# One hand-ordered schedule for a decode layer with its gradients: FFN weights read once in blocks, wo and K/V kept on chip, zero fills released step by step

## The chip, the cores and the metric

The kernel runs on one core of a Trainium2 chip. The metric is device time in microseconds, from runs of the whole program; the profile shows one execution of it. The core has five instruction queues that run side by side, each in its own order: TensorE (PE, with its weight loads as PEld), VectorE (DVE), ScalarE (ACT), GpSimd (POOL) and SyncE (SP). SP, ACT and POOL can issue DMA transfers between memory and the on-chip buffer; all of them run on the core's 16 DMA engines.

## The reference

One token passes a layer: modulation from `c`, attention of 32 query heads over the last 4096 rows of a cache with 4 K/V heads, a gated FFN. The outputs are the layer's output and the gradients of all inputs. Two of these, for the caches, have the size of the whole caches (65536 rows each), and are zero but for the last 4096 rows.

```python
W = min(4096, max(256, Sk // 4))
q = (x @ wq).reshape(B, Sq, Hq, Dh)
k = k_cache[:, :, Sk - W:, :] ; v = v_cache[:, :, Sk - W:, :]   # each K/V head serves 8 query heads
p = softmax(q k^T * Dh ** -0.5) ; o = p v
return o.reshape(B, Sq, Hq * Dh) @ wo                            # A_ref

h = sigmoid(x @ w_gate) * (x @ w_up)
return h @ w_down                                                # B_ref

sa, ca, ga, sb, cb, gb = (silu(c) @ w_mod).reshape(6, D)
h = layernorm(x) * (1 + ca) + sa ; x = x + ga * A_ref(h)
h = layernorm(x) * (1 + cb) + sb ; x = x + gb * B_ref(h)
# outputs: x, and the gradients of x, k_cache, v_cache, wq, wo, w_gate, w_up, w_down, c, w_mod
```

All is bfloat16. D is 1024, F 3584, wq 1024 x 4096, wo 4096 x 1024, w_mod 1024 x 6144.

## The kernel before

With one token there is hardly arithmetic: each weight is read, multiplied with a vector, and a gradient of its size, an outer product of two vectors, is written. A vector of 1024 stands as a column tile of 128 partitions x 8. Products with weights in the forward pass go to TensorE, with the weight as the stationary operand and one column as the moving one. Products in the backward pass (weight times gradient, summed along the rows) go to VectorE as one multiply-and-sum over a weight tile and a vector broadcast to all partitions: the helper `ttr` (L207), whose elementwise result goes to a scratch tile `junk`. The outer products are `outer_rows` (L211), also on VectorE, into staging tiles of the pool `stage` (2 buffers), which SP then stores. `bcast_from_col` (L202) makes the broadcast vectors: VectorE multiplies the identity with each column into `diag` (L200), TensorE multiplies with ones, ScalarE copies the result out of PSUM (L204).

The kernel's operations are written in the order of the layer; a scheduler orders each engine's queue from that, and pools decide which buffer a tile gets. The stages:

- POOL issues the 120 zero fills for the caches' gradients (L110), 1 MB each, at the start and one behind the other; eight may be in flight. Behind them in its queue stand small memsets, `dhh` (L405) among them.
- Modulation: w_mod in three tiles, 384 matmuls (L234). Query: wq in 8 tiles, 256 matmuls (L267).
- K is loaded and transposed (L297, copies L298), scores (L311), softmax, transposed probabilities (L336), V, output (L348). Then wo and 256 matmuls (L372), second norm.
- FFN: all of w_down (`wd`) and w_gate (`wg`) is loaded into the four slots of the pool `big`; the reductions of w_down (L207), 224 matmuls with w_gate (L423). w_up (`wu_t`) is streamed in 8 row tiles through 2 buffers (L441): matmuls (L444), reduction, outer product, store (L450). Then the w_gate reductions with their outer products (stored at L470), matmuls with w_down (L476), w_down's outer products (L486).
- Backward norm, four of the six w_mod sections (`wmod_section`, load L515, store L525), each reading its 1024 columns of w_mod again.
- wo is read again (`wo_r`), reduced, its gradient written (L545). K and V are read again (`k_sb2`, `v_sb2`), V transposed, gradients of V (L566, L570, stored at L574), the scores' gradient in two passes (L581, L589), gradients of K, the query's gradient (L348).
- wq is read again (`wqr`, L607), reduced, its gradient written (L616); backward norm; the last two w_mod sections.

## Time and profile before

| | us |
|---|---|
| median of 3 runs | 846.26 |
| lowest and highest run | 846.24 and 846.75 |
| span of the profiled execution, first to last instruction | 844.5 |
| DVE busy in it | 360.4 |
| PE busy | 173.9 |
| ACT busy | 101.8 |
| POOL busy | 65.4 |

The profile shows one execution. Its page gives the span in 40 equal slices (21.1 us each); a digit is the busy share of an engine in tenths, the row of the DMA engines gives their mean busy share, and the row under it what they moved in GB/s. A group row names line, engine, operation, output and inputs with their shapes, and after the bar the group's busy time, the mean duration of one in ns and the idle time before it with what ended it. A row of the timeline has its start and duration first. A window's row gives, behind its two times and its length, the busy time and count of PE, PEld, DVE, ACT and POOL, then TensorE's clock, the DMA engines' busy share and GB/s. The issue table gives for each group of transfers the size of one and the median time from issue to landing.

### The profile page before, as it was taken

The numbers are of one execution on the slowest core, as the hardware profiler recorded it, in microseconds if no ns is written. First come the engines' busy times: TensorE is split into PE (matmuls) and PEld (weight loads), VectorE is DVE, ScalarE is ACT, GpSimd is POOL, SyncE is SP. The second block draws the span as 40 slices with busy tenths as digits, with TensorE's granted clock in tenths as the row PEclk, the third lists the DMA queues.
The fourth block names the chain that finished last, engine by engine and source line by source line (L and its number), as shares of the span: only waits on it lengthen the run. The fifth ranks groups of instructions, "written<-read, shape, count | busy, mean of one in ns | idle before, by whom it ended". The sixth has DMA issues, their size and how long they took to land. (4 is left out here: it accounts for less than half of the span.)

```text
span 844.5 us, 7215 instructions
## 1 busy us (share of the span) xinstructions
PE 173.9 (21%) x2932; PEld 130.3 (15%) x2932; DVE 360.4 (43%) x680; ACT 101.8 (12%) x161; POOL 65.4 (8%) x136
## 2 busy tenths in 40 slices
PE   0211028310003000021002124021000057980032
PEld 0211025210003000021001123010000046560011
DVE  1100000300001000000399889997899940549986
ACT  0000006600000000000001001000100049460000
POOL 3111111111111111111100000000000000000000
PEclk9999999655555555555555555555555556555555
DMA  8999999999999999999931966888989996873423
GB/s 345 424 424 425 427 426 424 423 423 423 422 424 421 424 422 425 427 425 425 427 133 34 329 247 243 324 291 308 335 300 346 338 366 236 336 258 153 195 101 149
DMA packets 64749, 283.60 MB, mean 336 GB/s; under 512 B 4294, under 2 KB 4294, under 8 KB 43212
## 3 DMA queue, kind: packets, MB, share of 16 engines
q1 hardware_dynamic: 47436, 157.31, 49.5%
q0 software_dynamic: 17280, 125.84, 35.3%
q8 instruction: 23, 0.38, 0.2%
q14 instruction: 10, 0.08, 0.0%
HBM read 97.52 MB, written 185.60 MB: 335 GB/s over the span
## 5 line engine op out<-in xcount | busy, mean ns | idle before, releaser
L110 POOL DMA_DIRECT2D out_dram<-zeros x120 | 63.8, 533 | 348.6 <-DMA out_dram<-zeros 342.1
L207 DVE CUSTOM_DVE_ANT_0 junk<-wm_sec,dmod_b 128x1024 bf16<-128x1024 bf16 x48 | 58.4, 1218 | 2.8 <-ACT dmod_b L204 2.8
L202 PE MATMUL bc_ps<-diag,ones_bf 128*128 128x128 bf16 x152 | 31.1, 266 | 121.0 <-DVE diag L200 105.4
L456 DVE TENSOR_SCALAR omsg<-sg 128x28 f32<-128x28 f32 x1 | 0.2, 181 | 116.5 <-ACT sg L426 116.5
L207 DVE CUSTOM_DVE_ANT_0 junk<-wd,dffn_b 128x1024 bf16<-128x1024 bf16 x28 | 34.3, 1224 | 33.0 <-POOL dhh L405 32.2
L207 DVE CUSTOM_DVE_ANT_0 junk<-wo_r,dattn_b 128x1024 bf16<-128x1024 bf16 x32 | 38.8, 1211 | 0.0
L375 DVE COPY attn_col<-attn_ps 128x8 f32<-128x8 f32 x1 | 0.2, 167 | 87.3 <-PE attn_ps L372 87.3
L207 DVE CUSTOM_DVE_ANT_0 junk<-wqr,dq_b 128x4096 bf16<-128x4096 bf16 x8 | 35.3, 4417 | 1.1 <-issue 1.1
L202 PEld LDWEIGHTS <-ones_bf 128*128 128x128 bf16 x152 | 14.0, 107 | 133.3 <-issue 114.0
L207 DVE CUSTOM_DVE_ANT_0 junk<-wu_t,du_b 128x3584 bf16<-128x3584 bf16 x8 | 31.1, 3891 | 5.4 <-DMA wu_t<-in_B_w_up_dram 4.4
L207 DVE CUSTOM_DVE_ANT_0 junk<-wg,dg_b 128x3584 bf16<-128x3584 bf16 x8 | 31.1, 3883 | 0.4 <-ACT dg_b L204 0.4
L423 PE MATMUL g_ps<-h_bf,wg 128*128 128x1 bf16 x224 | 7.4, 166 | 110.5 <-DMA wg<-in_B_w_gate_dram 108.5
L298 ACT COPY kT_sb<-tp_kv 128x1024 bf16<-128x1024 bf16 x16 | 15.4, 1017 | 100.2 <-PE tp_kv L297 100.1
L566 PEld LDWEIGHTS <-P_bf 8*128 8x128 bf16 x256 | 25.1, 133 | 7.2 <-issue 4.6
L211 DVE TENSOR_SCALAR dwm_stg<-dmod_b,cs_col 128x1024 bf16<-128x1024 bf16 x48 | 22.6, 480 | 5.5 <-DMA out_dram<-dwd_stg 5.5
L204 ACT CAST dmod_b<-bc_ps 128x512 bf16<-128x512 f32 x12 | 6.7, 587 | 149.5 <-PE bc_ps L202 101.4
L372 PE MATMUL attn_ps<-o_bf,wo 128*128 128x1 bf16 x256 | 8.1, 166 | 79.6 <-DMA wo<-in_A_wo_dram 79.6
L423 PEld LDWEIGHTS <-wg 128*128 128x128 bf16 x224 | 6.7, 104 | 111.2 <-DMA wg<-in_B_w_gate_dram 109.2
L298 ACT COPY vT_sb<-tp_kv 128x1024 bf16<-128x1024 bf16 x16 | 15.3, 1028 | 65.5 <-PE tp_kv L297 65.5
L237 DVE COPY mod_col<-mod_ps 128x48 f32<-128x48 f32 x1 | 0.2, 208 | 51.5 <-PE mod_ps L234 51.5
L581 DVE CUSTOM_DVE_ANT_0 junk<-sc_ps,P_bf 128x512 bf16<-128x512 f32 x8 | 5.5, 692 | 35.3 <-PE sc_ps L311 34.3
L234 PE MATMUL mod_ps<-cs_bf,wm 128*128 128x1 bf16 x384 | 11.0, 165 | 46.1 <-DMA wm<-in_w_mod_dram 45.1
(190 smaller groups left out, 417.0 us busy)
## 6 DMA issues: line engine op xcount, KB each, us to landing
out_dram<-zeros POOLq DMA_DIRECT2D x120, 1024.0 KB, 25.7
wm<-in_w_mod_dram SPq DMA_DIRECT2D x6, 2048.0 KB, 34.4
wm_sec<-in_w_mod_dram SPq DMA_DIRECT2D x12, 1024.0 KB, 7.0
out_dram<-dwm_stg SPq DMA_DIRECT2D x12, 1024.0 KB, 5.0
wq<-in_A_wq_dram SPq DMA_DIRECT2D x8, 1024.0 KB, 44.9
k_sb<-in_A_k_cache_dram SPq DMA_DIRECT2D x8, 1024.0 KB, 23.5
v_sb<-in_A_v_cache_dram SPq DMA_DIRECT2D x8, 1024.0 KB, 18.9
wo<-in_A_wo_dram SPq DMA_DIRECT2D x8, 1024.0 KB, 49.6
```

The lines of the kernel that those rows point to most:

```text
L110: ins = zq.dma_start(out=region[:, i * ZW:i * ZW + w_], in_=zeros[:, :w_])
L202: nc.tensor.matmul(ps[:, jj * P:(jj + 1) * P], lhsT=ones_bf[:, :], rhs=dg_[:, :], start=True, stop=True)
L204: nc.scalar.copy(out=out_bf[:, j0 * P:(j0 + nj) * P], in_=ps[:, 0:nj * P])
L207: nc.vector.tensor_tensor_reduce(out=junk[:, 0:n], in0=w_ap, in1=b_ap, scale=1.0, scalar=0.0, op0=ALU.mult, op1=ALU.add, accum_out=acc_ap)
L211: nc.vector.tensor_scalar(out=stage_ap, in0=b_ap, scalar1=scal_ap, scalar2=None, op0=ALU.mult)
L234: nc.tensor.matmul(mod_ps[:, cidx:cidx + 1], lhsT=wm_sb[s][:, j, cc * P:(cc + 1) * P], rhs=cs_bf[:, j:j + 1], start=(j == 0), stop=(j == K ...
L237: nc.vector.tensor_copy(out=mod_col, in_=mod_ps[:, 0:KM])
L298: nc.scalar.copy(out=dst[:, g, tb * 1024:(tb + 1) * 1024], in_=tp[:, :])
L372: nc.tensor.matmul(attn_ps[:, cidx:cidx + 1], lhsT=wo_sb[h // 16][:, h % 16, cidx * P:(cidx + 1) * P], rhs=o_bf[:, h:h + 1], start=(h == 0 ...
L423: nc.tensor.matmul(g_ps[:, cidx:cidx + 1], lhsT=wg_j(j)[:, cidx * P:(cidx + 1) * P], rhs=h2_bf[:, j:j + 1], start=(j == 0), stop=(j == KD ...
L566: nc.tensor.matmul(ps[:, tt * DH:(tt + 1) * DH], lhsT=rows_bf[32 * g:32 * g + HG, t_ * P:(t_ + 1) * P], rhs=R_hd[32 * g:32 * g + HG, :], s ...
L581: nc.vector.tensor_tensor_reduce(out=junk[:, 0:512], in0=ps[:, 0:512], in1=P_bf[:, ch * 512:(ch + 1) * 512], scale=1.0, scalar=0.0, op0=AL ...
```

## The change

The kernel is written anew, in one order that the scheduler keeps (`manual_schedule`): each queue holds its instructions in the order of the code. Tiles have fixed places in one buffer, the arena.

- **Zero fills.** `zero(n, after)` puts the next `n` fills into POOL's queue, and each waits for the instruction `after` besides. There are 4 at the start, 38 more up to the FFN (after parts of the products with w_mod, wq and wo, and the transposes), 3 in each of the 7 FFN blocks, and 57 behind.
- **FFN in 7 blocks of 512 columns of F.** For each, one 1 MB tile of w_down, w_up and w_gate is loaded into five slots used in turn. Rows of the w_up and w_gate tiles are 1 KB in memory, those of w_down 8 KB. Forward and backward of a block follow each other: matmuls, sigmoids, reductions, broadcast, gradients. The reduction writes its elementwise result over the weight tile, the outer product over that, and the tile is stored from where it stands. The outer products of w_up and w_gate go to ScalarE (`outer_act`), which also issues their stores.
- **wo, K and V stay on chip.** Their second reads are gone; so is that of one of wq's 8 tiles. V's transposes take the place of K's in the forward pass.
- **w_mod** is read twice as before; in the backward pass in row tiles of 4096 columns through two slots, between the tiles of wq and behind them, and in tiles of 2048 columns at the end.
- **Smaller things.** The broadcast uses the column itself, repeated, as stationary operand, so that `diag` is gone. The memsets on POOL are gone. The scores' gradient is made in one pass, its row constant being taken from the outputs instead of the scores. The three input rows are loaded as one tile, the result rows are made with one transpose each.

Three places show what moved. The first is POOL's queue. Before, from the first fill on (`DMASW` are the semaphores of transfers issued by POOL, eight of them in turn):

```order
L110 DMA out_dram<-zeros 128x4096 [waits DVE_49]
L110 DMA out_dram<-zeros 128x4096 x7
L110 DMA out_dram<-zeros 128x4096 [waits DMASW0_49]
L110 DMA out_dram<-zeros 128x4096 [waits DMASW1_49]
L110 DMA out_dram<-zeros 128x4096 [waits DMASW2_49]
```

After, the fills of the first two FFN blocks and the first of the third:

```order
L119 DMA out_dram<-zeros 128x4096 [waits DMASW2_49,DVE_49]
L119 DMA out_dram<-zeros 128x4096 [waits DMASW3_49,Activation_49]
L119 DMA out_dram<-zeros 128x4096 [waits DMASW4_49,Activation_49]
L119 DMA out_dram<-zeros 128x4096 [waits DMASW5_49,DVE_49]
L119 DMA out_dram<-zeros 128x4096 [waits DMASW6_49,Activation_49]
L119 DMA out_dram<-zeros 128x4096 [waits DMASW7_49,Activation_49]
L119 DMA out_dram<-zeros 128x4096 [waits DMASW0_49,DVE_49]
```

Before, a fill waits only for the one eight places ahead of it. After, it waits for an instruction of another engine too.

The second is SP's queue in the FFN. Before, loads of w_up and stores of its gradient (`DMAHW` are the semaphores of transfers issued by SP and ACT):

```order
L441 DMA wu_t<-in_B_w_up_dram 128x3584 [waits DMAHW0_49,DMAHW2_49,DVE_49,PE_49]
L450 DMA out_dram<-dwu_stg 128x3584 [waits DMAHW3_49,DVE_49]
L441 DMA wu_t<-in_B_w_up_dram 128x3584 [waits DMAHW1_49,DMAHW4_49,DVE_49,PE_49]
L450 DMA out_dram<-dwu_stg 128x3584 [waits DMAHW5_49,DVE_49]
L450 DMA out_dram<-dwu_stg 128x3584 [waits DMAHW6_49,DVE_49]
L441 DMA wu_t<-in_B_w_up_dram 128x3584 [waits DMAHW7_49,DMAHW2_49,PE_49]
```

After, the store of a block's w_down gradient (L476), the loads of the next block's w_down, w_up and w_gate (L415, L418, L421), and the same for the block behind:

```order
L476 DMA out_dram<-arena 128x4096 [waits DMAHW6_49,DMAHW4_49,DVE_49]
L415 DMA arena<-in_B_w_down_dram 128x4096 [waits DMAHW5_49,DMAHW1_49,Activation_49]
L418 DMA arena<-in_B_w_up_dram 128x8x512 [waits DMAHW3_49,Activation_49]
L421 DMA arena<-in_B_w_gate_dram 128x8x512 [waits DMAHW4_49,DMAHW0_49,PE_49]
L476 DMA out_dram<-arena 128x4096 [waits DMAHW5_49,DMAHW2_49,DVE_49]
L415 DMA arena<-in_B_w_down_dram 128x4096 [waits DMAHW6_49,Activation_49]
L418 DMA arena<-in_B_w_up_dram 128x8x512 [waits DMAHW1_49,Activation_49]
L421 DMA arena<-in_B_w_gate_dram 128x8x512 [waits DMAHW2_49,PE_49]
```

The three loads now stand behind a store that waits for VectorE, and the load of w_gate waits for that store's landing as well, since it takes its slot.

The third is VectorE's queue in the FFN. Before, the last reduction with w_gate and its outer product, and the first outer products of w_down:

```order
L207 ISA junk_109,dh2g_2587<-wg1_1853,dg_b_2488 128x3584
L207 ISA dh2g_2587 128x1
L211 TENSOR_SCALAR dwg_stg_2618<-dg_b_2488,h2_1773 128x3584
L471 TENSOR_TENSOR dh2_2188<-dh2u_2189,dh2g_2587 128x8
L139 CAST x2_orow_2894<-ps_x2_0_2895 1x512
L211 TENSOR_SCALAR dwd_stg_2849<-dffn_b_1780,hh_2479 128x1024 x4
```

After, block 1 from its last reduction with w_down to the first one with w_up (`b1k` is the broadcast gradient, `dug` holds the gradients at the up and gate products):

```order
L151 ISA junk_1731,dhh1_1975<-arena_70,b1k_1710 128x1024
L151 ISA dhh1_1975 128x1
L134 TENSOR_TENSOR dug1_2016<-dhh1_1975,sg1_1971 128x4
L134 TENSOR_TENSOR dug1_2016<-dug1_2016,gu_ps_1906 128x4
L134 TENSOR_TENSOR dug1_2016<-dug1_2016,om1_1972 128x4
L143 CAST dug_bf1_2020<-dug1_2016 128x8
L147 TENSOR_SCALAR arena_70<-b1k_1710,hh1_1978 128x1024 x4
L151 ISA arena_70,dh2acc_1730<-arena_70,du_b_1732 128x512
L151 ISA dh2acc_1730 128x1
```

The outer products of w_up and w_gate are gone from this queue; the small products that need the block's sigmoids stand between the reductions.

The core of the diff:

```diff
-    for og in (out_2, out_3):
-        for g in range(G):
-            region = og[0, g, 0:SKW, :].rearrange("r d -> (r d)").rearrange("(p x) -> p x", p=P)
-            for i in range(nz):
-                ins = zq.dma_start(out=region[:, i * ZW:i * ZW + w_], in_=zeros[:, :w_])
+    def dep(later, earlier):
+        tc.add_manual_dep(later.ins, earlier.ins.name,
+                          mybir.DependencyInfo(mybir.DependencyClass.Sync, mybir.DependencyReason.DATA),
+                          reason="pace")
+    def zero(n, after=None):
+        for _ in range(n):
+            if not zleft:
+                return
+            ins = nc.gpsimd.dma_start(out=zleft.pop(0), in_=zeros[:, :])
+            if after is not None:
+                dep(ins, after)
...
-    for j in range(KD):
-        wu_t = stream.tile([P, F], BF16, tag="wstream", name="wu_t")
-        ld.dma_start(out=wu_t, in_=wu_view[:, j, :])
...
-        ttr(wu_t[:, :], du_b[:, :], dh2u[:, j:j + 1], F)
-        stg = stage.tile([P, F], BF16, tag="stg", name="dwu_stg")
-        outer_rows(stg, h2[:, j:j + 1], du_b[:, :])
-        st.dma_start(out=dwu_view[:, j, :], in_=stg)
+    def slot(i):
+        return ar(F_OFF + 8 * (i % 5), 8)
+    wd_t = [slot(3 * n) for n in range(NB)]
+    wu_t = [slot(3 * n + 1).rearrange("p (j f) -> p j f", j=KD) for n in range(NB)]
+    wg_t = [slot(3 * n + 2).rearrange("p (j f) -> p j f", j=KD) for n in range(NB)]
+    for n in range(NB):
...
+        for half, w in ((1, wu), (0, wg)):
+            for jj in range(4):
+                for j in range(KD):
+                    nc.tensor.matmul(gu[:, half * 4 + jj:half * 4 + jj + 1], lhsT=w[:, j, jj::4],
+                                     rhs=h2_bf[:, j:j + 1], start=(j == 0), stop=(j == KD - 1))
+        nc.scalar.activation(out=sg, in_=gu[:, 0:4], func=ACT.Sigmoid)
...
+        last = cp(dug_bf, dug)
+        zero(1, last)
...
+        for jj in range(4):
+            outer_dve(wd[:, jj, :], hh[:, jj:jj + 1], b1k)
+        nc.sync.dma_start(out=wd_dram(out_8, n), in_=wd_t[n])
+        for j in range(KD):
+            ttr(wu[:, j, :], wu[:, j, :], du_b, dh2acc[:, n * 16 + j:n * 16 + j + 1])
+            last = outer_act(wu[:, j, :], h2[:, j:j + 1], du_b)
+        nc.scalar.dma_start(out=dwu_view[:, :, n * FB:(n + 1) * FB], in_=wu)
+        zero(1, last)
+        if n + 1 < NB:
+            if n + 1 > 1:
+                load_wd(n + 1)
+            load_wu(n + 1)
+        for j in range(KD):
+            ttr(wg[:, j, :], wg[:, j, :], dg_b, dh2acc[:, n * 16 + 8 + j:n * 16 + 9 + j])
+            last = outer_act(wg[:, j, :], h2[:, j:j + 1], dg_b)
+        nc.scalar.dma_start(out=dwg_view[:, :, n * FB:(n + 1) * FB], in_=wg)
+        zero(1, last)
+        if n + 1 < NB:
+            load_wg(n + 1)
...
-    wo_sb2 = load_wo("wo_r")
-    for h in range(HQ):
-        ttr(wo_sb2[h // 16][:, h % 16, :], dattn_b[:, :], do_col[:, h:h + 1], D)
+    for q4 in range(8):
+        for hh4 in range(4):
+            h = q4 * 4 + hh4
+            w = wo_t[q4][:, hh4, :]
+            ttr(w, w, dattn_b, do_col[:, h:h + 1])
+            last = outer_act(w, o_col[:, h:h + 1], dattn_b)
+        nc.scalar.dma_start(out=dwo_view[:, q4 * 4:(q4 + 1) * 4, :], in_=wo_t[q4])
+        zero(2, last)
...
-    k_sb2 = load_kv(A_k_cache, "k_sb2")
-    v_sb2 = load_kv(A_v_cache, "v_sb2")
-    vT_sb = transpose_kv(v_sb2, "vT_sb")
...
+    for j in range(KD):
+        ttr(wq_t[j], wq_t[j], dq_b, dh1[:, j:j + 1])
+        grad_kv(gkv[8 * j:8 * j + 8])
+        last = outer_dve(wq_t[j], h1[:, j:j + 1], dq_b)
+        nc.sync.dma_start(out=dwq_view[:, j, :], in_=wq_t[j])
+        zero(1, last)
+        if j % 2 == 1 and j < 6:
+            k = j // 2
+            sec_ttr(k)
+            last = sec_outer(k, "V")
+            zero(1, last)
+            sec_load(k + 2)
...
+    for k in range(3, KD):
+        sec_ttr(k)
+        last = sec_outer(k, "V")
+        zero(2, last)
+        if k + 2 < KD:
+            sec_load(k + 2)
+    zero(200, last)
+    for j in range(KD):
+        ttr(s2_t[j], s2_t[j], dmod_b2, dcs[:, KD + j:KD + j + 1])
+        outer_act(s2_t[j], cs_col[:, j:j + 1], dmod_b2)
+        nc.scalar.dma_start(out=dwm_view[:, j, 0:2048], in_=s2_t[j])
```

More of the change, by code (lines that the diff above doesn't have):

```diff
@@ L20 @@
 F = 3584
-KF = F // P
+FB = 512
+NB = F // FB
 HQ = 32
@@ new lines, in av_like @@
+        return ps, mm
+    pT = transpose_rows(P_bf, "pT")
+    o_ps, mm = av_like(v_nat, pT, "o")
+    zero(2, mm)
+    o_col = vt([P, HQ], "o_col")
+    cp(o_col, o_ps[:, 0:HQ])
+    o_bf = vt([P, HQ], "o_bf", BF16)
+    cp(o_bf, o_col)
+    attn_ps = new_acc("attn_ps")
+    for h in range(HQ):
+        for k in range(KD):
+            mm = nc.tensor.matmul(attn_ps[:, k:k + 1], lhsT=wo_t[h // 4][:, h % 4, k * P:(k + 1) * P],
+                                  rhs=o_bf[:, h:h + 1], start=(h == 0 and k == 0), stop=(h == HQ - 1),
+                                  skip_group_check=True)
+        if h % 4 == 3:
+            zero(1, mm)
```

836 lines of the change are left out of this document (385 added, 451 removed).

## The prediction

> **What bounds the kernel now.** I read the page's slices first, then the same span cut in two, then the chain.
>
> ```profile
> span 844.5 us, 7215 instructions
> DVE  1100000300001000000399889997899940549986
> POOL 3111111111111111111100000000000000000000
> DMA  8999999999999999999931966888989996873423
> GB/s 345 424 424 425 427 426 424 423 423 423 422 424 421 424 422 425 427 425 425 427 133 34 329 247 243 324 291 308 335 300 346 338 366 236 336 258 153 195 101 149
> ```
> ```profile
> 0.00:420.00 420.00, 65.78 (x1636) 54.45 (x1637) 22.32 (x74) 32.79 (x41) 65.38 (x136) 0.68 1.01 420
> 420.00:844.50 424.50, 108.09 (x1296) 75.85 (x1295) 338.08 (x607) 68.97 (x120) 0.00 (x0) 0.51 0.69 252
> ```
> ```profile
> DVE 16%; PE 6%; ACT 2%; issue 2%; DMA 1%; DVEq 0%; ACTq 0%
> ```
>
> There are two kernels in one span. For 420 us the DMA engines are full at 420 GB/s while DVE works 22 us; for the other 424 us DVE is busy 338 us (80%), the 16 DMA engines carry 252 GB/s, and the chain of waits runs over DVE. POOL's row shows why they split: all zero fills are issued in the first half, when DVE has nothing to do, and the second half has none left to fill its gaps. Merging the halves is what can pay.
>
> ```profile
> q1 hardware_dynamic: 47436, 157.31, 49.5%
> q0 software_dynamic: 17280, 125.84, 35.3%
> HBM read 97.52 MB, written 185.60 MB: 335 GB/s over the span
> out_dram<-zeros POOLq DMA_DIRECT2D x120, 1024.0 KB, 25.7
> wo_r<-in_A_wo_dram SPq DMA_DIRECT2D x8, 1024.0 KB, 7.1
> k_sb<-in_A_k_cache_dram SPq DMA_DIRECT2D x8, 1024.0 KB, 23.5
> v_sb<-in_A_v_cache_dram SPq DMA_DIRECT2D x8, 1024.0 KB, 18.9
> wqr<-in_A_wq_dram SPq DMA_DIRECT2D x8, 1024.0 KB, 8.1
> ```
>
> Zero fills are 125.8 of the 283.1 MB read and written, 120 of 1.049 MB each. After the change POOL's queue holds nothing else behind its start, so a fill that waits for its release holds up later fills and no one else. (Before, memsets stood behind all fills, and DVE waited 32.2 us for one, `dhh`; they are gone.)
>
> **The change part by part.** *Bytes.* Gone are the second reads of wo (8 issues), of K and V (4 of each 8) and of one wq tile: 17 × 1.049 = 17.8 MB. 283.1 − 17.8 = 265.3 MB stay. Zero fills and gradients are written as before. At the 424 GB/s that the full slices show, 265.3 MB take 626 us; nothing in the change can go below that. The question is how much of the span the queues stay full.
>
> *Who gets the bandwidth when zero fills are queued.* Four rows each from the timeline, during the loads of wq (8 KB rows) and of wo (2 KB rows), each tile 1.049 MB:
>
> ```profile
> 106.33 0.19 PE L267 MATMUL q_ps<-h_bf,wq 128*128 128x1 bf16 x1 [4.72 <-DMA wq<-in_A_wq_dram]
> 111.24 0.19 PE L267 MATMUL q_ps<-h_bf,wq 128*128 128x1 bf16 x1 [4.72 <-DMA wq<-in_A_wq_dram]
> 109.37 0.53 POOL L110 DMA_DIRECT2D out_dram<-zeros  x1 [4.34 <-DMA out_dram<-zeros]
> 114.30 0.53 POOL L110 DMA_DIRECT2D out_dram<-zeros  x1 [4.41 <-DMA out_dram<-zeros]
> ...
> 185.11 0.53 POOL L110 DMA_DIRECT2D out_dram<-zeros  x1 [2.65 <-DMA out_dram<-zeros]
> 185.26 0.27 PE L372 MATMUL attn_ps<-o_bf,wo 128*128 128x1 bf16 x4 [11.20 <-DMA wo<-in_A_wo_dram]
> 188.22 0.53 POOL L110 DMA_DIRECT2D out_dram<-zeros  x1 [2.58 <-DMA out_dram<-zeros]
> 197.04 0.27 PE L372 MATMUL attn_ps<-o_bf,wo 128*128 128x1 bf16 x4 [11.51 <-DMA wo<-in_A_wo_dram]
> ```
>
> With equal rows a load gets a tile per 4.9 us and a zero fill takes 4.9 us: half and half. With 2 KB rows the load gets a tile per 11.8 us against a zero fill per 3.1 us. So a queued zero fill pushes aside loads with short rows, the more the shorter; the 1 KB rows of the new wu and wg blocks come off worst. No byte is lost by that, but the compute that waits for such a load is late.
>
> *Front, up to the first FFN block.* It loads w_mod (12.6 MB), wq, K and V, wo (8.4 each) and three FFN tiles (3.1), 40.9 MB, and releases 42 zero fills (44.0 MB): 84.9 MB, 200 us at 424. Does compute fit in? Before, K's transposes to the attention output took this long, and attention projection and norm the rest:
>
> ```profile
> 130.50 0.39 PE L297 MATMUL tp_kv<-ident_bf,k_sb 128*128 128x128 bf16 x2
> 173.25 0.19 DVE L353 COPY o_col<-av_o 128x32 f32<-128x32 f32 x1 [9.15 <-PE av_o L348]
> 254.66 6.24 PE L372 MATMUL attn_ps<-o_bf,wo 128*128 128x1 bf16 x228 [11.19 <-DMA wo<-in_A_wo_dram]
> 260.94 0.17 DVE L375 COPY attn_col<-attn_ps 128x8 f32<-128x8 f32 x1 [87.28 <-PE attn_ps L372]
> 265.30 0.17 DVE L188 CAST h_bf<-h 128x8 bf16<-128x8 f32 x1
> ```
>
> 43 us, then 6 us of matmuls behind the last wo tile, then 4.4 us: 54 us after q. By bytes q is there when w_mod, wq and 20 zero fills are through (42 MB, 99 us), so 101 us are left for 54 us of work: the front stays bound by DMA, 200 us, and no zero fill is left over for the FFN loop.
>
> *FFN loop, 7 blocks.* DVE per block, from these rows:
>
> ```profile
> L207 DVE CUSTOM_DVE_ANT_0 junk<-wd,dffn_b 128x1024 bf16<-128x1024 bf16 x28 | 34.3, 1224 | 33.0 <-POOL dhh L405 32.2
> L581 DVE CUSTOM_DVE_ANT_0 junk<-sc_ps,P_bf 128x512 bf16<-128x512 f32 x8 | 5.5, 692 | 35.3 <-PE sc_ps L311 34.3
> L207 DVE DVE_READ_ACCUMULATOR2_ANT dhh<- 128x1 f32 x28 | 2.3, 81 | 0.0
> L211 DVE TENSOR_SCALAR dwd_stg<-dffn_b,hh 128x1024 bf16<-128x1024 bf16 x28 | 11.7, 479 | 0.1
> L572 ACT ACTIVATE stg_dk<-ps_dk 128x512 bf16<-128x512 f32 x32 | 16.2, 644 | 14.0 <-PE ps_dk L566 14.0
> 495.16 0.91 PE L444 MATMUL u_ps<-h_bf,wu_t 128*128 128x1 bf16 x28 [6.37 <-DMA wu_t<-in_B_w_up_dram]
> 470.00:500.00 30.00, 4.52 (x140) 4.12 (x140) 24.32 (x21) 0.00 (x0) 0.00 (x0) 0.50 0.95 348
> ```
>
> Four reductions of 1024 columns (4 × 1.30), 16 of 512 (16 × 0.77, the 512-column row standing in), four wd outer products (1.9), six small ones (1.1 at the 0.17 to 0.19 of the short rows above): 20.5 us. The wu and wg outer products leave DVE for ScalarE: 16 × 0.64 us (the 512-column row there), 10 us beside it, hidden as long as ScalarE stays under DVE. DMA per block: six tiles and three zero fills, 9.44 MB, 22.3 us at 424. So 22.3 us is the lower bound.
>
> The upper one comes from SP's queue. Its four transfers of a block (store wd, load the next wd, wu, wg) all stand behind the wd store, which waits for DVE's outer products; and the wg load also waits for that store to land, since it takes its slot. Four tiles at the half share of 4.9 us are 19.6 us; then come 32 matmuls (28 took 0.91, so 1.0), two sigmoids, hh and its cast (0.8 at the same 0.2 each), two reductions (2.6), the small products (0.7) and the outer products (1.9): 26.6 us from one set of outer products to the next, against 20.5 us of DVE work. The wu loop of before, which also turned loads and stores through few buffers, moved 348 GB/s with its DMA engines 0.95 busy; 9.44 MB at that rate are 27.1 us. I take 27, since two ways agree. Three fills a block last 9.3 us; in that time a load at half share moves 1.9 tiles, at wo's pace 0.8. The shortfall, 1.1 tiles, is 5.4 us: 32, and 33 for rows half as long as wo's. Seven blocks: 189 (156 to 231).
>
> *Rest.* 265.3 − 84.9 − 62.9 (seven blocks less the three tiles loaded) = 117.5 MB, 57 zero fills among them: 277 us at 424. DVE's work there:
>
> ```profile
> L207 DVE CUSTOM_DVE_ANT_0 junk<-wqr,dq_b 128x4096 bf16<-128x4096 bf16 x8 | 35.3, 4417 | 1.1 <-issue 1.1
> L211 DVE TENSOR_SCALAR dwq_stg<-dq_b,h 128x4096 bf16<-128x4096 bf16 x8 | 10.2, 1279 | 0.0
> L589 DVE SCALAR_TENSOR_TENSOR P_bf<-sc_ps,crow,P_bf 128x512 bf16<-128x512 f32 x8 | 5.4, 741 | 0.1
> ```
>
> 32 × 1.30 for wo, 16 × 5.7 for wq and w_mod's wide part, 8 × 2.3 for its narrow part (half of 4.4, and 0.1), 5.4 for dS, and by estimate 35 for norms, broadcasts, transposes and the 256-column products between: 191 us. That leaves 86 us of slack for SP's stores and reloads of two w_mod slots. So DMA binds again, with some 9 us where it cannot be full (the norm after the FFN, the last reductions and row). 286; lower 277. Upper: the hardware queue alone moved 106.7 MB (424 us at 252) while busy 0.69 of the time, 365 GB/s; 57.7 MB at that and 59.8 MB of zeros at 422 are 300 + 9 = 309.
>
> Sum: 200 + 189 + 286 = 675 us of span. Before's span is 844.5 where the runs' median is 846.3, so 1.8 us lie around it: 677.
>
> *A rule that speaks against the change.* Zero fills are now issued while DVE works. Each issue:
>
> ```profile
> L110 POOL DMA_DIRECT2D out_dram<-zeros x120 | 63.8, 533 | 348.6 <-DMA out_dram<-zeros 342.1
> ```
>
> 78 of them fall behind the front, 41 us of POOL in 475. The trace of before has hardly any zero fill beside a DVE scalar product, so a collision shows nowhere. The longest such product is 1.28 us (the wq row); if every late issue waited for one, POOL would be busy 141 us of 475, and nothing would be late. The Trainium skill, page "SBUF — State Buffer", section "SBUF: two separate sides", says that a DMA issued from GpSimd cannot get its descriptors written while DVE runs a two-port operation, and advises the other queues. If the fills stood still for all scalar products behind the front, 28 × 0.48 + 16 × 1.28 = 34 us, the time would be 711; eight fills in flight cover 20 us, so I keep 677.
>
> **The rivals.**
>
> *Full throughout* (the blocks' turn hidden by released fills): 626 + some 12 for start and end = 638. For: the first half held 420 GB/s with loads and fills. Against: the SP order above.
>
> *Lower rate with loads and stores mixed:* from 200 us on the engines move 348 GB/s although busy, as in 470 to 500. 180.4 / 0.348 = 518, in all 720. Against: the first half mixed 125.8 MB of writes with 50 MB of reads at 420. The Trainium skill, page "DMA: Bandwidth & Descriptors", section "Bandwidth", names about 358 GB/s as what binds between HBM and SBUF; all 265.3 MB would then be 741 us. The first 420 us at 420 GB/s do not agree with that.
>
> *Longer turn:* 33 us a block, 719.
>
> *Slower than before:* the releases come too late. Every fill behind the front hangs on an instruction that itself waits for a load; if a load is late, the fills are late too, and the queues run dry together. Place: FFN loop and rest; price: before's second-half rate, 252 GB/s, 180.4 / 0.252 = 716, in all 918. It decides once the mean rate after 200 us falls under 180.4 / 646 = 279 GB/s. For it: that half ran at that rate. Against: it had no fill left, and 78 now stand behind 200 us.
>
> *The change does not do what it says:* a release is only an earliest time. If fills pile up, loads are pushed aside as wo's were; that is the upper end of the rest, 309.
>
> **How the numbers follow.** Forecast (655 to 705) 0.57; full throughout 0.15; lower rate 0.12; longer turn 0.09; stopped fills 0.03; slower 0.03; about as before 0.01. The range 640 to 722 leaves out half of the full case, half of the two rivals around 720 and the slower one: 0.57 + 0.07 + 0.11 + 0.03, about 8 in 10. A measurement tells 0.2% (1.7 us) from no change. Faster 0.96, same 0.01, slower 0.03.
>
> **What would show it.** Right: GB/s near 420 up to about 200 us, then 330 to 400 with dips in each FFN block, DVE waiting there for a wg load by way of the sigmoid; block period 27; read bytes 79.7 MB; fills to the end. Wrong: period at 22 (the turn is hidden) or over 31; slices under 300 GB/s behind the FFN; zero issues much longer than 0.53 us.

## The result, and the profile after

The changed kernel takes 720.29 us (median of 4 runs, 718.67 to 720.63) against 846.25 for the kernel before (843.98 to 846.75): a ratio of 0.8509, 95% interval 0.8488 to 0.8531. The forecast was 677, so direction and most of the gain were there and 43 us of the gain were not. First the rows of the page that answer to those of before.

```profile
span 718.1 us, 6808 instructions
POOL 2001101120100000000000021102100110000000
...
DMA  8999999999969788797968699999999999997896
GB/s 347 428 426 425 427 425 427 416 421 416 417 251 377 273 321 309 270 365 249 381 209 325 241 412 422 398 407 419 416 420 425 413 418 417 412 422 281 323 384 270
...
HBM read 79.70 MB, written 185.60 MB: 369 GB/s over the span
...
DMA 69%; DVE 16%; PE 6%; ACT 5%; issue 2%; SPq 1%; ACTq 1%; DVEq 0%
```

POOL's row, empty behind its middle before, has work there now (the last zero fill is issued at 694 us, by the row of L119 further down), and 17.8 MB of reads are gone, as forecast. The chain, which ran over DVE in a second half before, now runs over DMA for 69%. But the GB/s row has two weak places: slices 12 to 23 (the FFN loop), at 209 to 381, and the last four. The span cut in stretches (columns: span, busy time and instructions of PE, PEld, DVE, ACT, POOL, then PE's granted clock, DMA share, GB/s):

```profile
0.00:200.00 200.00, 62.36 (x1365) 55.32 (x1365) 30.57 (x78) 29.59 (x35) 24.22 (x50) 0.86 1.01 416
209.40:393.50 184.10, 26.59 (x624) 23.94 (x624) 103.16 (x300) 74.41 (x120) 10.07 (x18) 0.50 0.83 303
408.90:450.00 41.10, 1.62 (x10) 1.27 (x10) 39.08 (x81) 19.55 (x20) 6.85 (x13) 0.50 1.02 411
450.00:650.00 200.00, 52.71 (x544) 40.82 (x544) 85.86 (x76) 58.26 (x98) 20.66 (x39) 0.53 1.01 415
650.00:718.10 68.10, 0.38 (x1) 0.08 (x1) 35.96 (x32) 16.01 (x8) 3.16 (x6) 0.50 0.82 308
```

The front is nearly as forecast, 416 GB/s up to 200 us: 83.2 MB, 1.7 less than its sum had. The six FFN blocks from the first `hh` to the last carry 303 GB/s at a DMA share of 0.83. The rest is full up to 650 us, then falls to 308 at 0.82. Against the forecast's sum: front 200 (right); FFN loop from 200 to the copy of `ffn` at 408.9, 209 for 189; rest 309 for 286. One FFN block, in the timeline and then in stretches:

```profile
328.97 0.16 DVE L134 TENSOR_TENSOR hh<-sg,gu_ps 128x4 f32<-128x4 f32 x1 [13.15 <-ACT om L445]
332.81 0.62 POOL L119 DMA_DIRECT2D out_dram<-zeros  x1 [17.13 <-DVE dug_bf L143]
...
334.13 0.36 SPq L476 DMA_DIRECT2D out_dram<-arena  x1
...
334.59 1.21 SPq L415 DMA_DIRECT2D arena<-in_B_w_down_dram  x1
335.89 1.65 SPq L418 DMA_DIRECT2D arena<-in_B_w_up_dram  x1
340.41 0.38 ACTq L480 DMA_DIRECT2D out_dram<-arena  x1
340.67 0.53 POOL L119 DMA_DIRECT2D out_dram<-zeros  x1 [7.24 <-ACT arena L155]
340.82 0.38 SPq L421 DMA_DIRECT2D arena<-in_B_w_gate_dram  x1
345.92 0.38 ACTq L489 DMA_DIRECT2D out_dram<-arena  x1
346.19 0.53 POOL L119 DMA_DIRECT2D out_dram<-zeros  x1 [4.98 <-ACT arena L155]
361.30 0.16 DVE L134 TENSOR_TENSOR hh<-sg,gu_ps 128x4 f32<-128x4 f32 x1 [14.45 <-ACT om L445]
```
```profile
328.00:334.00 6.00, 2.69 (x60) 2.28 (x58) 4.83 (x14) 1.01 (x3) 0.62 (x1) 0.50 0.05 18
334.00:358.00 24.00, 1.20 (x32) 1.14 (x32) 12.37 (x37) 11.38 (x18) 1.06 (x2) 0.50 1.03 372
...
360.00:366.00 6.00, 3.02 (x70) 2.61 (x68) 4.49 (x14) 0.69 (x3) 0.62 (x1) 0.50 0.01 3
```

For six microseconds around the block's start, and again around the next one's, almost no transfer runs (shares 0.05 and 0.01). Everything that could be in flight, the three fills included, is released by the new block's own products, and these wait for one load. The chain of waits names it; each piece of it is start, duration, what:

```profile
334.13 6.62 DMA out_dram<-arena
340.82 18.84 DMA arena<-in_B_w_gate_dram
```

Store of the w_down tile 6.6 us, load of the w_gate tile into its slot 18.8, then 6.8 of matmuls and products: 32.3 us for one turn, from store to store. The chain names the same two pieces in the blocks around it, with stores of 6.5 to 6.6 us and w_gate loads of 12.6 in the first turn and 17.5 to 18.8 in the others. From 200 to 409 us the DMA engines are dark (share under 0.3) in 41 of 209 one-microsecond windows.

The end, on SyncE's queue and on POOL:

```profile
618.25 17.87 SPq L650 DMA_DIRECT2D arena<-in_w_mod_dram  x8
638.87 0.34 SPq L536 DMA_DIRECT2D out_dram<-arena  x1
661.59 0.33 SPq L526 DMA_DIRECT2D arena<-in_w_mod_dram  x1
```
```profile
633.34 0.54 POOL L119 DMA_DIRECT2D out_dram<-zeros  x1 [2.49 <-issue]
674.26 1.05 POOL L119 DMA_DIRECT2D out_dram<-zeros  x2 [40.38 <-DVE arena L147]
...
693.57 1.05 POOL L119 DMA_DIRECT2D out_dram<-zeros  x2 [10.69 <-DVE arena L147]
```

A wide w_mod tile's store goes out at 638.87, behind eight narrow loads, though DVE had ended its product at 604.3; it also stood behind a load at 613.26 that waited for another store to land. The load that takes its slot can start only at 661.59, and the last six fills wait for the products of the tiles behind it: POOL issues nothing from 634 to 674 us.

### The profile page after: what moved, and what is told of

The parts are those of the page before. It is cut to its first block, busy times and chain, and to the rows that moved or that the text cites. A ratio compares the mean times of both kernels' runs of the same rounds, so it can differ in the third digit from the quotient of the medians.

```text
span 718.1 us, 6808 instructions
## 1 busy us (share of the span) xinstructions
PE 148.1 (21%) x2648; PEld 125.4 (17%) x2648; DVE 309.3 (43%) x610; ACT 208.7 (29%) x298; POOL 66.1 (9%) x128
## 4 chain that ended last, share of the span: by engine, by line
DMA 69%; DVE 16%; PE 6%; ACT 5%; issue 2%; SPq 1%; ACTq 1%; DVEq 0%
DMA out_dram<-arena 25%; DMA arena<-in_B_w_gate_dram 19%; DMA arena<-in_w_mod_dram 8%; DVE arena L151 8%; DMA arena<-in_A_wq_dram 6%; DMA arena<-in_A_k_cache_dram 5%; DMA arena<-in_A_wo_dram 4%; ACT arena L155 4%; DVE junk L151 2%; DVE arena L147 2%; PE tp_kv L309 2%; PE bc_ps L208 1%; ACT arena L312 1%; PE gu_ps L440 1%; DVE mx L330 1%
## 5 line engine op out<-in xcount | busy, mean ns | idle before, releaser
L151 DVE CUSTOM_DVE_ANT_0 arena<-arena 128x4096 bf16<-128x4096 bf16 (+1 forms) x24 | 88.5, 3709 | 97.0 <-DMA arena<-in_w_mod_dram 96.8
L119 POOL DMA_DIRECT2D out_dram<-zeros x120 | 65.0, 543 | 627.8 <-ACT arena L155 148.1
L440 PE MATMUL gu_ps<-h_bf,arena 128*128 128x1 bf16 x448 | 16.9, 172 | 152.0 <-DMA arena<-in_B_w_up_dram 102.5
L155 ACT ACTIVATE arena<-b1k,o_col 128x1024 bf16<-128x1024 bf16 x32 | 34.4, 1138 | 38.3 <-issue 15.5
L440 PEld LDWEIGHTS <-arena 128*128 128x128 bf16 x448 | 16.0, 117 | 154.1 <-issue 131.5
L151 DVE CUSTOM_DVE_ANT_0 arena<-arena,b1k 128x1024 bf16<-128x1024 bf16 x32 | 36.7, 1217 | 0.0
L151 DVE CUSTOM_DVE_ANT_0 arena<-arena,du_b 128x512 bf16<-128x512 bf16 x56 | 34.8, 686 | 3.1 <-ACT du_b L473 3.1
L155 ACT ACTIVATE arena<-dg_b,h 128x512 bf16<-128x512 bf16 x56 | 35.0, 708 | 3.7 <-DVE dh2acc L151 3.7
L155 ACT ACTIVATE arena<-du_b,h 128x512 bf16<-128x512 bf16 x56 | 34.9, 710 | 0.0
L151 DVE CUSTOM_DVE_ANT_0 arena<-arena,dg_b 128x512 bf16<-128x512 bf16 x56 | 34.8, 685 | 0.0
L151 DVE CUSTOM_DVE_ANT_0 junk<-arena,b1k 128x1024 bf16<-128x1024 bf16 x28 | 34.2, 1222 | 0.5
L309 PE MATMUL tp_kv<-ident_bf,arena 128*128 128x128 bf16 x256 | 22.3, 254 | 23.5 <-DMA arena<-in_A_k_cache_dram 15.6
L309 PEld LDWEIGHTS <-arena 128*128 128x128 bf16 x256 | 19.4, 116 | 26.3 <-DMA arena<-in_A_k_cache_dram 16.5
```

Source lines behind the costliest of these rows:

```text
L119: ins = nc.gpsimd.dma_start(out=zleft.pop(0), in_=zeros[:, :])
L151: return nc.vector.tensor_tensor_reduce(out=out, in0=w, in1=b, scale=1.0, scalar=0.0, op0=ALU.mult, op1=ALU.add, accum_out=acc)
L155: return nc.scalar.activation(out=out, in_=b, func=ACT.Copy, scale=col)
L309: nc.tensor.transpose(tp[:, t8 * P:(t8 + 1) * P], src[:, g, t_ * DH:(t_ + 1) * DH], ident_bf[:, :])
L440: nc.tensor.matmul(gu[:, half * 4 + jj:half * 4 + jj + 1], lhsT=w[:, j, jj::4], rhs=h2_bf[:, j:j + 1], start=(j == 0), stop=(j == KD - 1))
```

## The experiments

*Four on the FFN loop.* Three theories stand against each other, named in the first expectation: A, fills push the short-row loads aside; B, short rows are slow by themselves; C, the turn through SyncE's queue and the slots. The first run takes the fills out of it:

```diff
         last = cp(dug_bf, dug)
-        zero(1, last)
...
-    zero(4, last)
+    zero(9, last)
...
         nc.scalar.dma_start(out=dwo_view[:, q4 * 4:(q4 + 1) * 4, :], in_=wo_t[q4])
-        zero(2, last)
+        zero(4, last)
```
(and the two other `zero(1, last)` of a block.)

> The 21 fills that are released inside the seven FFN blocks are released behind the loop instead (nine at its end, four rather than two per wo tile); nothing else changes, all bytes stay. In the changed kernel a block takes 30.7 us. Theory A, fills push the short-row loads aside: the blocks fall to the reductions' own pace, 21 to 24 us, about 50 us less for the loop, and the 21 fills come back at 2.5 us each behind it, 52 us; the time stays within 10 us of 720. Theory B, 1 KB rows go slowly whoever else is there: a block of the changed kernel keeps its engines busy 25.7 us (31 at 0.83), 12.4 of these for five 8 KB-row tiles at 2.47, so a 1 KB-row tile costs 3.3; without fills 18.3 us of transfers are left, and the blocks go to 23 to 25 as well. Theory C, the turn through SyncE's queue and five slots is what takes the time, with or without fills: 28 to 31 and a time of about 760.

The second gives the loads long rows:

```diff
+    def chunk(t, n):
+        flat = t.rearrange("r c -> (r c)")
+        return flat[n * P * 4096:(n + 1) * P * 4096].rearrange("(p j f) -> p j f", p=P, j=KD)
...
-        nc.sync.dma_start(out=wg_t[n], in_=wg_view[:, :, n * FB:(n + 1) * FB])
+        nc.sync.dma_start(out=wg_t[n], in_=chunk(B_w_gate, n))
```
(and w_up likewise.)

> The loads of the w_up and w_gate tiles take the same number of bytes as one contiguous piece, 8 KB a row instead of eight rows of 1 KB, so the tiles hold other weights than they should and the FFN's results change; stores keep their 1 KB rows, order and fills stay. Theory A (pushed aside): the two loads now get their full share against a fill; blocks of 24 to 27 us, time 675 to 695. Theory B (1 KB rows cost engine time): two of the four short-row tiles get 0.9 us cheaper, blocks of 29, time 708. Theory C (turn): blocks of 30 to 31, time 715 to 720.

The third moves two loads on SyncE:

```diff
+        if n + 1 < NB:
+            if n + 1 > 1:
+                load_wd(n + 1)
+            load_wu(n + 1)
         nc.sync.dma_start(out=wd_dram(out_8, n), in_=wd_t[n])
```
(and they are gone from behind the w_up gradient.)

> On SyncE the loads of the next w_down and w_up tiles, whose slots the block before gave back, stand ahead of the w_down store instead of behind it; only the w_gate load, which takes the w_down tile's slot, stays behind. Theory C (turn): the w_gate load has no load beside it and lands within 10 to 12 us instead of 17.5; blocks of 24 to 27, time 675 to 695. Theory A: three fills still pass it, blocks of 28 to 31, time 700 to 720. On the other side: the loads now wait for the stores of the block before, and the w_down store behind them with them, so the w_gate load may go out later; then 31 to 34 and a time up to 740.

The fourth gives the slots out otherwise:

```diff
-    wd_t = [slot(3 * n) for n in range(NB)]
+    wd_t = [slot(0) for n in range(NB)]
...
-        nc.sync.dma_start(out=wd_dram(out_8, n), in_=wd_t[n])
+        nc.scalar.dma_start(out=wd_dram(out_8, n), in_=wd_t[n])
+        if n + 1 < NB:
+            load_wu(n + 1)
+            load_wg(n + 1)
+            load_wd(n + 1)
```
(w_up in slot 1 or 3, w_gate in 2 or 4, by turns; the loads of before, behind the gradients, are gone.)

> The five slots are given out otherwise: the w_down tile has one slot of its own, w_up and w_gate two each, and the w_down store goes out on ScalarE's queue. The two 1 KB-row loads of the next block are then issued a block ahead, and the late load is the w_down tile with its 8 KB rows. Theory C (turn): blocks of 22 to 25 us, time 660 to 680. Theory A: the fills still push the 1 KB-row loads aside, but they have a whole block to land, so blocks of 24 to 27. Theory B: transfers of 25.7 us a block bound it, blocks of 26, time 685.

Measured: the time; the mean of the six blocks between the first and the last `hh`; the median from issue to landing of a w_gate load; the ratio to the kernel before with its 95% interval.

| kernel | time, us | block, us | w_gate load, us | ratio to before |
|---|---|---|---|---|
| changed kernel | 720.29 | 30.7 | 17.5 | 0.8509 (0.8488 to 0.8531) |
| x1, no fills in the loop | 705.37 | 22.6 | 11.2 | 0.8331 (0.8308 to 0.8354) |
| x2, 8 KB-row loads | 684.25 | 25.4 | 13.0 | 0.8084 (0.8056 to 0.8111) |
| x3, loads ahead of the store | 696.80 | 27.6 | 8.5 | 0.8249 (0.8217 to 0.8281) |
| x4, w_down turns | 684.86 | 25.5 | 11.0 | 0.8091 (0.8066 to 0.8115) |

The seven `hh` of each, x1 to x4 in this order (shortest, median and longest duration in ns, then the first and the last start, whose distance is six blocks), with the stretch between them:

```profile
L134 DVE TENSOR_TENSOR hh<-sg,gu_ps x7: 157/158/159, 209.3 to 344.8; 128x4 f32<-128x4 f32 x7
209.30:344.80 135.50, 26.57 (x624) 23.94 (x624) 103.16 (x300) 74.46 (x120) 0.00 (x0) 0.50 0.79 272
```
```profile
L134 DVE TENSOR_TENSOR hh<-sg,gu_ps x7: 157/158/159, 203.0 to 355.6; 128x4 f32<-128x4 f32 x7
203.00:355.60 152.60, 26.56 (x624) 23.93 (x624) 103.13 (x301) 74.44 (x120) 10.06 (x18) 0.50 0.98 367
```
```profile
L134 DVE TENSOR_TENSOR hh<-sg,gu_ps x7: 157/158/159, 209.4 to 374.9; 128x4 f32<-128x4 f32 x7
209.40:374.90 165.50, 26.05 (x624) 24.16 (x624) 103.21 (x301) 74.71 (x121) 10.06 (x18) 0.50 0.91 333
```
```profile
L134 DVE TENSOR_TENSOR hh<-sg,gu_ps x7: 151/152/159, 209.6 to 362.3; 128x4 f32<-128x4 f32 x7
209.60:362.30 152.70, 26.25 (x624) 24.39 (x624) 103.13 (x299) 74.65 (x120) 10.02 (x18) 0.50 0.98 359
```

Theory A holds: without fills the w_gate load lands in 11.2 us and the block falls to 22.6 (theory B allowed 23 to 25 there, so this run alone hardly parts the two); with rows of 8 KB in 13.0 and the block to 25.4, in the same order on SyncE and from the same slots. Theory B alone cannot explain x2 (it asked for 29). Theory C holds beside it: x3 and x4 leave rows and fills as they are and gain all the same, x4 as much as x2 (35.4 and 36.0 us), x3 two thirds of that (23.5). In x4 the short-row loads take slots that the block before gave back, and the late load is the w_down tile's, with rows of 8 KB; in x3 the w_gate load goes out 15 us behind its block's w_up load (242.27 and 257.61), not beside it. So it takes both: a load with short rows that is last in the block's turn, and fills that pass it. With long rows, or with the short-row loads out early, the engines stay lit (share 0.98 in x2 and x4). The Trainium skill, page "DMA: Bandwidth & Descriptors", section "Queues, rings and completion order", says that each DMA engine takes turns between the queues a packet of descriptors at a time; we infer that a queue with longer rows moves more bytes in its turn, and 17.5 against 13.0 us agrees with that. x3 gains less, since its other side came true as well: the loads on SyncE now wait for the stores of the block before, and the w_down store behind them. In its second block DVE ends the w_down products at 232.80 and the store goes out at 242.73, behind a w_up load at 242.27.

In x1 the engines are dark as before (0.79, with a third fewer bytes in the loop), yet the kernel gains. The loop loses 48.7 us (`ffn` is copied at 360.2, not 408.9), and the 21 fills come back for 34.8 us, 1.7 each, not 2.5: they fill a part of the hole at the end, whose last 64 us now carry 390 GB/s. That beat the expectation of no change by 15 us.

*Three on the end and on the fills.* Places of their own for the wide tiles:

```diff
-        return ar(F_OFF + 24 + 8 * (j % 2), 8)
+        return ar([F_OFF + 24, F_OFF + 32, A_OFF + 56, E_OFF, A_OFF, A_OFF + 8, A_OFF + 16, A_OFF + 24][j], 8)
```
(`sec_load(2)` behind the wq reloads, `sec_load(j + 2)` behind the wq tiles 1 to 5.)

> The eight wide w_mod tiles of the end get a place of their own each (two as now, the 8 KB that wo leaves free, and the wq tiles that were already written back), so none waits for the store of another; fills and the FFN loop stay. In the changed kernel the last 68 us carry 308 GB/s where 200 us before them carry 415: 17.5 us of transfer time are lost there. Theory D, the turn of two slots makes that hole: the last stretch is full, 700 to 706. Theory E, the hole is there because the last ten fills hang on the last five tiles and come too late: loads come earlier, the fills stay late with the tiles' scalar products, 712 to 720; the products themselves come earlier, so a part of D is left even so. On the other side: loads that come earlier push the wq reloads aside by up to 5 x 2.5 us, 720 to 730.

Narrow loads later:

```diff
-    for j in range(KD):
-        nc.sync.dma_start(out=s2_t[j], in_=wm_view[:, j, 0:2048])
     for k in range(3, KD):
...
+        for j in ([], [], [], [0, 1], [2, 3], [4, 5], [6, 7], [])[k]:
+            nc.sync.dma_start(out=s2_t[j], in_=wm_view[:, j, 0:2048])
```

> The eight narrow w_mod loads (0.5 MB each) stand on SyncE behind the wide tiles' stores and loads instead of ahead of them. Theory F, SyncE's order makes the hole at the end: the 4.2 MB no longer stand in front of the wide store and load, each turn is up to 10 us shorter at the first one, 706 to 712. Theory D (two slots): the turn stays, 715 to 722, or up to 730 if the narrow loads are then late for their own loop.

Fills without a release:

```diff
             ins = nc.gpsimd.dma_start(out=zleft.pop(0), in_=zeros[:, :])
-            if after is not None:
-                dep(ins, after)
```

> The fills are no longer released step by step: all 120 are issued as fast as GpSimd's queue takes them, as in the kernel before; the rest of the schedule stays. If the step-by-step release carries the gain: fills take half of the engines or more until they are through (some 120 x 3 to 4 us, at about 400 us), wo and the FFN tiles come at 8 to 13 us each, the first FFN blocks take 40 us and more, and the rest has no fill for its gaps: 760 to 800. If single pass and kept tiles carry it and the release little: 700 to 735, since the fill-free FFN blocks run at 22.6 us, as measured.

x5 took 716.84 us (0.8483, 0.8466 to 0.8500), x6 711.49 (0.8420, 0.8378 to 0.8462), x7 739.48 (0.8750, 0.8730 to 0.8771). So the two slots (theory D) are worth at most 2 to 4 us, not 14 to 20, and x5's interval meets the changed kernel's (0.8488 to 0.8531): that gain is not clear of noise. SyncE's order (F) is worth 7 to 9. The time of x5 also lies where theory E (the fills come too late) put it, 712 to 720; but x5 issues its last fill at 661.74, ahead of the hole that is left. Where x5's gain went is seen on SyncE: the five wide stores, ready one by one as the products end, all wait behind the narrow loads.

```profile
626.83 30.59 SPq L652 DMA_DIRECT2D arena<-in_w_mod_dram  x8
660.58 15.33 SPq L536 DMA_DIRECT2D out_dram<-arena  x5
```
```profile
680.00:700.00 20.00, 0.38 (x1) 0.08 (x1) 7.25 (x13) 9.36 (x5) 0.00 (x0) 0.50 0.80 336
700.00:714.00 14.00, 0.00 (x0) 0.00 (x0) 0.00 (x0) 4.33 (x3) 0.00 (x0) 0.50 0.41 168
```

The hole has moved to the last 34 us, where only stores are left. In x7 the last fill is issued at 414.5 us:

```profile
200.00:400.00 200.00, 15.72 (x366) 14.20 (x367) 39.31 (x119) 27.25 (x44) 33.15 (x63) 0.50 1.02 421
400.00:600.00 200.00, 39.16 (x750) 32.36 (x749) 132.05 (x349) 103.49 (x146) 3.08 (x6) 0.53 0.78 289
600.00:737.60 137.60, 34.74 (x282) 27.37 (x280) 112.00 (x84) 50.81 (x77) 0.00 (x0) 0.51 0.78 294
```

421 GB/s, then 289 and 294: the picture of before, two kernels in one span. Theory A shows once more inside this run: the chain's w_gate load takes 46.1 us beside an unbroken row of fills (issued at 286.27), and 11.1 to 12.1 once they are through (from 459.87 on). Yet the whole costs only 19 us of the 126 gained. So in this schedule the step-by-step release is the small part of the gain; the other 107 us come with the rest of the rewrite (single pass, kept tiles, gradients in place, outer products on ScalarE), whose parts were not tried one by one.

*The parts together, and the rate.* x8 joins x4 and x5; x11 also puts the narrow loads on ScalarE's queue:

```diff
-        nc.sync.dma_start(out=s2_t[j], in_=wm_view[:, j, 0:2048])
+        nc.scalar.dma_start(out=s2_t[j], in_=wm_view[:, j, 0:2048])
```

x9 and x10 are x4 with 8 KB rows in the two stores or in the two loads, x12 is x11 with both (`chunk` as in x2, with `out_6` and `out_7` for the stores).

> The two edits x4_turn and x5_slots together. If the losses of the FFN loop and of the end are separate, their gains add: 685 less 17 is 668 (theory D), 680 to 685 by theory E. If the end is only the place where a common debt of bytes is paid, the sum is less than the parts.

> x4_turn with the w_up and w_gate gradients written as contiguous pieces, 8 KB a row instead of eight rows of 1 KB; the same bytes go to other places of these two outputs, which are wrong thereby. In x4_turn the engines are busy 0.98 of the FFN loop at 359 GB/s, so its 25.5 us a block are transfer time; 9.44 MB at 424 would be 22.3. The 3.2 us must be paid by the 1 KB rows of two loads, of two stores, or by mixing loads and stores as such. If stores pay: blocks of 22.5 to 24, time 665 to 675. If loads pay, or the mixing: blocks of 25 to 25.5, time 682 to 686.

> x4_turn with the w_up and w_gate loads as contiguous pieces of 8 KB rows (other weights in the tiles, so the FFN's results change). If loads pay for 1 KB rows: blocks of 22.5 to 24, time 665 to 675. If stores pay: blocks of 24.7 to 25.5, time 680 to 686. If the mixing pays: 25.5, time 685 in both this and the run with contiguous stores.

> The version that the runs point to: the slots of x4_turn, the places of x5_slots, and the narrow w_mod loads on ScalarE's queue, so that the wide stores on SyncE no longer stand behind them. In x8_turn_slots the last 34 us carry 320 GB/s, 8 us of transfer time lost. If SyncE's order makes that hole: 672 to 676. If the hole is only the last stores draining: 678 to 681.

> x11_all with loads and stores of w_up and w_gate as contiguous pieces (results changed as in the two runs above). It asks for the floor: 265.3 MB at 424 GB/s are 626 us, 638 with start and end. If the short rows are what keeps the schedule off that floor: 640 to 655, blocks of 22 to 23.5. If loads and stores mixed run at 360 to 370 GB/s whatever the rows: 670 to 678, blocks of 25.5.

| kernel | time, us | ratio to before |
|---|---|---|
| x8, slots of x4 and x5 | 679.54 | 0.8048 (0.8013 to 0.8083) |
| x9, x4 with 8 KB-row stores | 684.67 | 0.8116 (0.8075 to 0.8157) |
| x10, x4 with 8 KB-row loads | 681.71 | 0.8066 (0.8032 to 0.8101) |
| x11, all together | 676.64 | 0.8007 (0.7983 to 0.8032) |
| x12, x11 with 8 KB rows | 675.91 | 0.7996 (0.7974 to 0.8018) |

x11 is the fastest of those that change nothing in the computation, 44 us under the changed kernel. Its FFN loop and rest, and x12's loop:

```profile
207.30:360.40 153.10, 26.40 (x624) 24.47 (x624) 103.08 (x299) 74.79 (x120) 10.02 (x18) 0.50 0.99 361
400.00:600.00 200.00, 53.48 (x544) 41.91 (x544) 116.58 (x113) 58.90 (x99) 21.83 (x38) 0.52 1.01 408
600.00:640.00 40.00, 0.38 (x1) 0.08 (x1) 22.13 (x26) 12.95 (x7) 3.73 (x7) 0.50 1.02 426
```
```profile
202.90:363.70 160.80, 25.56 (x624) 24.80 (x624) 103.14 (x299) 74.81 (x120) 10.03 (x18) 0.50 0.91 352
```

The gains of x4 and x5 are in keeping with a sum (35.4 and 3.5 us; x8 has 40.8 of the changed kernel's 720.3), but x8's interval overlaps x4's, so the second part is not shown. x11 against x8 is not told apart either: their intervals touch, and its time lies between its two expectations. The hole at the end is still there, 322 GB/s over x11's last 32.6 us where x8's last 34 carry 320, so taking the narrow loads off SyncE did not close it.

Engines that are full carry 361 GB/s in x11's loop and 408 to 426 behind it. The expectation that long rows would lift the loop to 424, and the time to 640 to 655, fell: x12 is no faster than x11. Two things are in that. Its loop is not full, the share is 0.91 and a block takes 26.8 us. The wait that ends its turn is the one of x11, DVE's for the w_down load, 53.2 us in all against 45.7:

```profile
L151 DVE CUSTOM_DVE_ANT_0 junk<-arena,b1k 128x1024 bf16<-128x1024 bf16 x28 | 34.2, 1223 | 53.6 <-DMA arena<-in_B_w_down_dram 53.2
```

And for each unit of share its engines carry 387 GB/s (352 / 0.91) against 365 (361 / 0.99): long rows give back 22 GB/s, a third of the 60 that lack to 424. x9 and x10, each with one kind of row, show 684.7 and 681.7 us against 684.9, with blocks of 26.4 and 25.7, where 665 to 675 was expected if that kind paid. In x9 the long rows of the stores push the short-row loads aside in their turn: its w_gate load lands after 18.6 us (median), x4's after 11.0.

The table of DMA queues, taken over the two loops, says where the rest lies (packets, MB, share of the 16 engines' time; `q1` is SyncE's queue, `q10` ScalarE's). ScalarE's line of x11 and both lines of x12:

```profile
q10 hardware_dynamic: 12734, 18.27, 32.7%
```
```profile
q1 hardware_dynamic: 2514, 18.33, 32.4%
q10 hardware_dynamic: 2515, 18.38, 27.7%
```

By MB over share and length, ScalarE's queue, which has the stores alone, goes from 365 GB/s (two of three stores with 1 KB rows) to 413 with long rows: that is a price of the short rows themselves, theory B's in small. SyncE's queue, which has the loads alone, reaches only 352 with long rows (347 in x11), where the same queue made 407 in the changed kernel's front (40.66 MB in half of 200 us). So what slows busy engines in the loop beyond the rows is mostly time in the loads (the zero fills make 397 in x12's loop, 421 in the front). Mixing loads and stores as such does not do it: the front mixes both at 416. In x12 two weak windows lie where a load has just been issued (w_up at 274.45; a store and a fill went out just before it):

```profile
274.00:276.00 2.00, 0.00 (x0) 0.00 (x0) 0.00 (x0) 0.24 (x2) 0.53 (x1) 0.50 0.89 270
276.00:278.00 2.00, 0.00 (x0) 0.00 (x0) 0.00 (x0) 0.00 (x0) 0.00 (x0) 0.50 0.82 274
...
280.00:282.00 2.00, 0.00 (x0) 0.10 (x1) 0.12 (x1) 0.00 (x0) 0.00 (x0) 0.50 1.02 434
```

At a share of 0.82 to 0.89 they carry 270 GB/s there, and 434 four microseconds later. The same dip, 266 to 274, stands behind the w_up loads at 220.06, 246.76 and 300.90, but not behind the one at 330.29 (418 and more), so a load's start alone does not make it. Why the loads go slowly there was not tried by itself and stays open.

## Why the prediction was right in sign and 43 us short

720.29 us lies inside the stated range by 1.7 us and outside the band of the forecast itself, 655 to 705. The range reached to 722 for the sake of two rivals near 720, so that it held is owed to them and not to the sum. Of the signs of being wrong two came: slices under 300 GB/s behind the FFN (281 and 270, the hole at the end), and one issue of a zero fill much longer than 0.53 us; the block's 30.7 stayed just under the 31 that was named.

*Bytes and front:* right. 79.7 MB were read, and 200 us went by at 416 GB/s with no fill left over.

*FFN block, 27 forecast, 30.7 measured.* The step that failed is "I take 27, since two ways agree". The first way gave all four SyncE transfers the half share of 4.9 us, 19.6 together. In the block shown the w_down store took 6.6, and the w_gate load behind it 18.8: 25.4. The upper bound of the same paragraph, 32 to 33 with fills passing the short rows, was the better reading, and the forecast had the rule for it from wq's and wo's rows: the shorter the row, the more is pushed aside. x2 shows that size: 5.3 us a block, of which the price of the two loads' short rows themselves is a small part (by estimate 0.7 us, two tiles at 365 rather than 413 GB/s). The second way, 348 GB/s, agreed by chance: 303 GB/s is 0.83 of the time at 365, dark for the other sixth.

*What became of the fills as a cover.* The forecast let three fills a block lie beside the turn. They do not, since each hangs on a product behind the late load. That is the slower rival in small: load late, fills late, queues dry together, six microseconds at a time. Its price of 252 GB/s and its threshold of 279 were not reached: 200 to 718 us carry 352 GB/s (265.7 less 83.2 MB in 518 us).

*Rest, 286 forecast, 309 measured.* Three terms. The stretches behind 408.9 us carry 120.9 MB (16.9 + 83.0 + 21.0), 3.4 more than the 117.5 of the sum, since front and loop had carried less than theirs: 8 us that were owed. At 411 to 415 GB/s rather than 424 they need some 7 more. The remaining 8 are the hole at the end: 68.1 us at 308 rather than 415 lose 17.5, of which 9 were allowed. "86 us of slack for SP's stores and reloads of two w_mod slots. So DMA binds again" held up to 650 us. It left out what stands between store and reload on SyncE: 4.2 MB of narrow loads (x6: 7 to 9 us; x5: the slots alone 2 to 4, not clear of noise).

*Rivals.* *Longer turn* (33 us a block, 719) named the mechanism of the loop, but not the rest's share. *Lower rate* (720) has the right time for half a reason: engines that are full in the loop do carry only 359 to 367 GB/s (x4, x2), near the 358 that the Trainium skill, page "DMA: Bandwidth & Descriptors", section "Bandwidth", names as what binds; but front and rest run at 411 to 416, nearer the 425 that the same section gives as measured on a single core, so no limit of 358 holds here. Of the six blocks' loss (184.1 us at 303 would be 131.6 at 424) dark engines are 31 us and the rate 21. *Full throughout* (638) was reached by no run: x11, full up to 660 us, takes 676.6. Its six blocks' 153.1 us at 361 would be 130.4 at 424, and its 200 us at 408 would be 192.5: 30 of the 39 us between. *Releases that do nothing:* x7 prices them at 19 us.

*Zero fills beside DVE's scalar products.* An issue takes 543 ns on average, against 533 before; the longest is new.

```profile
L119 POOL DMA_DIRECT2D out_dram<-zeros x120: 531/531/1216, 3.3 to 694.1; - x120
```

The longest, 1.22 us, runs from 143.21 to 144.43 us, in the front, beside a scalar product of 4096 columns on DVE from 143.03 to 144.32, and ends 0.11 us after it. This one agrees with the Trainium skill's rule (page "SBUF — State Buffer", section "SBUF: two separate sides"). Behind the front no issue took more than 0.62 us. All 120 took 1.2 us more of POOL than before, and no chain runs over that: keeping 0 was right.

## What to carry to other kernels

Ask of a double-buffered loop which transfer is issued last and has the shortest rows: that one lands last when long-row traffic is queued beside it, and when it does land nothing else may be left in flight; give the late slot to the tile with the long rows. Filler traffic covers a gap only if its release does not hang on the work that the gap delays. Read GB/s together with the DMA share: a low rate at a low share is a wait that reordering can remove, while a low rate at full share is a price that reordering leaves.

## What the runs showed of the hardware

The landing time of a 1 MB load with 1 KB rows was 17.5 us beside three 8 KB-row fills and two stores, 11.2 without the fills, 13.0 with 8 KB rows (medians of the changed kernel, x1 and x2). Full DMA engines carried from 359 GB/s (x4's FFN loop) to 426 (x11, 600 to 640 us), and row length moved the loop's rate by 22 for each unit of share (x12 against x11): ScalarE's queue of stores made 365 GB/s for its share of the engines with 1 KB rows in two of three stores, and 413 with 8 KB rows in all. A fill's issue took up to 1.22 us, 0.67 before, with a median of 0.53 in both; the longest ended 0.11 us after the scalar product on VectorE beside it.
